# First attention batch by pairs of heads in a fused pooled-attention and MoE kernel

## The chip, the cores and the metric

The kernel runs on one core of one Trainium2 chip. The metric is the device time of one launch in microseconds. A core has five engines with their own instruction lists: TensorE (PE, matmul; its weight loads are PEld), VectorE (DVE), ScalarE (ACT), GpSimd (POOL) and SyncE (SP), which issues most of the transfers. Each list is executed in order; engines wait for one another and for transfers through semaphores.

## The reference

All data is float32. There are 8 batches, 8 heads, 576 positions, 64 features of a head; the hidden layer has 2048 features.

```python
# attention with pooled keys and values (pool = 8, so Sp = 72)
k_p = k.reshape(B, H, Sp, 8, D).mean(axis=3)
v_p = v.reshape(B, H, Sp, 8, D).mean(axis=3)
scores = 1/sqrt(D) * q @ k_p.T
scores = scores - max(scores, axis=-1)
attn = exp(scores)
attn = attn / (sum(attn, axis=-1) + 1e-09)
x = (attn @ v_p)            # transposed to [B*S, H*D] = [4608, 512]
# hidden layer and output
h = x @ w_in                # 512 x 2048
s = sin(alpha * h)
g = h + s * s / (alpha + 1e-09)
out = g @ w_out             # 2048 x 512
```

## The kernel before

The kernel has three stages. `first_batch` computes the attention of batch 0 as fast as it can. Then nine units `u` of 512 tokens of the hidden layer run, each in 28 slots of one product (a Strassen-like scheme: four groups J of w_in, seven products each; p is the number of the product). Into these slots `carry(u)` puts the attention of the next batch. Last come the output products. A product is four matmuls of 128x128 by 256, which the profile shows as eight records.

The first batch, shortened:

```python
def first_batch(self):
    far = [self.home(i, [P, 2, 2, POOL * self.D]) for i in (1, 2)]
    ...
    self.load_alpha(...); self.turn_alpha()
    for i in range(4):                          # k of batch 0, pooled on VectorE
        self.load_kv("k", 0, i, nc.vector, at=far[i // 2][:self.Sp, i % 2])
    self.root()                                 # sqrt(1/alpha): Sqrt table
    self.load_q(0)                              # q of all heads in one transfer of 1 MB
    self.load_v_rows(0, ...)
    self.load_w_in(); self.load_w_in_part(0)
    self.pairs_q(0, range(5))                   # copies q so that two heads lie side by side
    A.k_t(); A.new_a(); A.q_t(0); A.q_t(1)      # transposes of k, of q's tiles of 128 rows
    v = self.sum_v_rows(0)
    ps = A.products(0)
    A.q_t(2)
    for i in range(4):                          # by tile of 128 rows, all heads
        A.soft(i, ps)                           # maximum, exp
        if i < 3:
            ps = A.products(i + 1)
            if i < 2:
                A.q_t(i + 3)
            next(v)
        if i:
            A.norm(i - 1)                       # row sum, reciprocal, multiply on GpSimd
    A.a_t(0, 0); A.a_t(0, 1); A.norm(3); A.a_t(1, 0); A.a_t(1, 1)
    for i in range(4):
        self.load_kv("k", 1, i)                 # k of batch 1: load, pool on GpSimd
    self.load_q(1)
    self.load_w_in_part(1)
    ...                                         # a_t of tiles 2 and 3
    self.combine_w_in(0, 0); self.combine_w_in(0, 1)
    for hp in range(4):
        A.values(hp)
    self.sums_of_x(0, 0); self.sums_of_x(0, 1)
```

`load_kv` issues a transfer into one of three `kvin` buffers and adds it up in three steps on GpSimd:

```python
def load_kv(self, n, b, i, eng=None, at=None):
    t = self.kvp.tile([Sp, 2, POOL * D], F32, name="kvin") if at is None else at   # kvp: bufs=3
    nc.sync.dma_start(out=t, in_=src[b, 2 * i:2 * i + 2]...)
    for w in (4 * D, 2 * D, D):
        o = t[:, :, 0:w] if w > D else to[b][:, 2 * i:2 * i + 2, :]
        (eng or nc.gpsimd).tensor_tensor(out=o, in0=t[:, :, 0:w], in1=t[:, :, w:2 * w], op=OP.add)
```

The first slots of unit 0 (`at(slot, f, ...)` puts f ahead of the product of that slot):

```python
at(0, self.sums_of_x, u, 2); at(0, self.sums_of_x, u, 3)
at(1, lambda: A0.soft(4, A0.products(4)))       # the last 64 rows of batch 0
at(2, A0.norm, 4)
at(5, A0.a_t, 4, 0); at(5, A0.a_t, 4, 1)
at(7, A0.values_rest)
at(0, self.load_w_in_part, 2)
for J in range(1, 4):
    at((4, 10, 14)[J - 1], self.combine_w_in, J, 0)   # sums of w_in's blocks, VectorE
    at((6, 12, 15)[J - 1], self.combine_w_in, J, 1)
at(6, self.load_w_in_part, 3)
at(3, self.pairs_q, 1, (0, 1)); at(4, self.pairs_q, 1, (2, 3, 4))
for i in range(5):
    at(5 + i, A.q_t, i)
at(7, A.k_t)
...
# in hidden(): the products of the slots are p = 1, 5, 6, 2, 7, 3, 4. Left over to the next slot:
def left0(): nc.scalar.copy(out=G.b6[:], in_=G.b1[:])
def left2(): nc.scalar.copy(out=G.b7[:], in_=G.b6[:]); nc.scalar.copy(out=G.p5[:], in_=G.b5[:])
def left3(): sin(G, 0, 0, G.b1); square(G, 0, 0)
def left4(): add(G.g[:, 1, :, 1], G.b7[:], G.p5[:])   # must read b7 before p = 4 adds to it
def left5(): add(G.g[:, 0, :, 1], G.b6[:], G.p5[:]); sin(G, 1, 1, G.g[:, 1, :, 1]); ...
```

## Time and profile before

| what | value |
|---|---|
| median of 3 runs | 939.52 us (939.14 to 941.21) |
| span of the profiled execution | 937.9 us |
| first product of the hidden layer starts | 33.45 us |
| fourth k load of batch 1 issued | 32.44 us |
| VectorE's combine of w_in group 1 starts, having waited 3.00 us for a transfer | 45.22 us |
| product of slot 6 (p = 4) starts | 47.45 us |
| ScalarE table loads until 45 us | 1.18, 3.98, 17.24, 43.18 us, 1.28 us each |

A busy share is an average over stages. What bounds a stage is read from the chain that ended last, which goes back from the last instruction, at each step to what released it. `LNNN` is the line of the program; a name such as `kvin<-in_k_dram` is what is written and what is read.

### The profile page before, as it was taken

How to read it: one execution, taken by the hardware profiler on the slowest of the kernel's cores; microseconds unless marked ns; L12 is line 12 of the kernel's file. 1: busy time of each engine (PE TensorE's matmuls, PEld its weight loads, DVE VectorE, ACT ScalarE, POOL GpSimd, SP SyncE). 2: the span in 40 equal slices, each digit the busy share in tenths (PEclk: the TensorE clock that was granted, in tenths of full speed). 3: DMA queues.
4: the chain of work that ended last, by engine and by line, in shares of the span. 5: the costliest groups of instructions: out<-in, count | busy, mean ns of one | idle time of the engine just before them, and what ended most of it. 6: DMA issues, size and time to landing. Idle time of an engine off the chain costs nothing.

```text
span 937.9 us, 17446 instructions
## 1 busy us (share of the span) xinstructions
PE 916.1 (98%) x6819; PEld 814.8 (87%) x6819; DVE 691.3 (74%) x1036; ACT 444.3 (47%) x1022; POOL 200.1 (21%) x216
## 2 busy tenths in 40 slices
PE   5998999999999999999999999999999999999997
PEld 3687787878878788787888899999999999999997
DVE  5788574867748676483456889988889798889794
ACT  5557585775867758677696641112121111111111
POOL 1738262553625435260000000000000000000000
PEclk9999999999999999999999999999999999999999
DMA  8574557666576664745525446253535444343501
GB/s 234 158 215 145 145 156 194 200 159 191 152 187 214 140 188 113 183 139 159 215 88 170 161 140 176 78 168 86 164 90 149 106 136 118 123 131 98 155 14 38
DMA packets 139777, 137.82 MB, mean 147 GB/s; under 512 B 49024, under 2 KB 108176, under 8 KB 139696
## 3 DMA queue, kind: packets, MB, share of 16 engines
q1 hardware_dynamic: 138624, 135.53, 50.1%
q10 hardware_dynamic: 1072, 1.19, 0.5%
q8 instruction: 54, 0.88, 0.4%
q14 instruction: 27, 0.22, 0.1%
HBM read 74.46 MB, written 47.19 MB: 130 GB/s over the span
## 4 chain that ended last, share of the span: by engine, by line
PE 93%; DVE 3%; DMA 2%; ACT 1%; issue 1%; SPq 1%; POOL 0%; DVEq 0%; ACTq 0%; POOLq 0%
PE bank L484 44%; PE bank L764 29%; PE ps_y L764 12%; PE ps_o L304 3%; PE ps_sc L210 2%; DMA q<-in_q_dram 1%; DMA a<-in_moe_w_in_dram 1%; PE ps_qt L191 1%; PE ps_at L261 0%; DVE sm L251 0%; DVE h L463 0%; PE ps_or L313 0%; PE bank L122 0%; DVE as L366 0%; DVE a L366 0%
## 5 line engine op out<-in xcount | busy, mean ns | idle before, releaser
L484 PE MATMUL bank<-home,a 128*128 128x256 f32 x1152 | 267.1, 383 | 2.3 <-DVE h L463 1.5
L484 PEld LDWEIGHTS bank<-home,a 128*128 128x128 f32 x1152 | 214.8, 190 | 37.3 <-DVE h L463 3.6
L484 PE MATMUL bank<-home,as 128*128 128x256 f32 x864 | 202.2, 382 | 0.2
L484 PEld LDWEIGHTS bank<-home,as 128*128 128x128 f32 x864 | 161.3, 190 | 25.1 <-ACT bank L510 3.0
L107 POOL TENSOR_TENSOR kvin<-kvin 72x512 f32<-72x512 f32 x112 | 123.2, 1100 | 162.7 <-DMA kvin<-in_v_dram 106.5
L764 PE MATMUL bank<-s,wb 128*128 128x144 f32 x896 | 119.4, 286 | 0.4 <-ACT bank L877 0.4
L764 PEld LDWEIGHTS bank<-s,wb 128*128 128x128 f32 x896 | 113.7, 190 | 0.7 <-ACT bank L877 0.6
L497 ACT ACTIVATE s<-s,c 128x256 f32<-128x256 f32 (+1 forms) x216 | 110.0, 572 | 0.0
L490 ACT ACTIVATE s<-h,al 128x256 f32<-128x256 f32 x144 | 65.3, 501 | 79.5 <-DVE h L463 79.4
L463 DVE TENSOR_TENSOR h<-bank,p 128x512 f32<-128x512 f32 x72 | 49.2, 683 | 60.1 <-ACT s L497 25.4
L877 ACT COPY bank<-bank 128x144 f32<-128x144 f32 x56 | 14.7, 263 | 145.7 <-PE bank L764 144.3
L490 ACT ACTIVATE s<-bank,al 128x256 f32<-128x256 f32 x144 | 60.0, 467 | 33.8 <-PE bank L484 10.5
L551 DVE TENSOR_TENSOR h<-bank,s 128x512 f32<-128x512 f32 x36 | 24.6, 684 | 49.1 <-ACT s L497 48.4
L244 POOL TENSOR_TENSOR ex<-ex,sm 128x576 f32<-128x576 f32 (+1 forms) x40 | 45.0, 1149 | 55.5 <-DVE sm L243 30.7
L896 ACT COPY bank<-bank 128x144 f32<-128x144 f32 x56 | 14.7, 263 | 88.5 <-PE bank L764 88.5
L719 DVE TENSOR_TENSOR s<-r 128x576 f32<-128x576 f32 x64 | 48.1, 752 | 0.8
L551 DVE TENSOR_TENSOR h<-h,s 128x1024 f32<-128x1024 f32 x36 | 46.5, 1292 | 0.0
L719 DVE TENSOR_TENSOR s<-x 128x576 f32<-128x576 f32 x48 | 36.2, 754 | 7.6 <-PE ps_y L764 6.7
L854 ACT COPY bank<-ps_y 128x288 f32<-128x288 f32 x56 | 21.5, 383 | 38.7 <-PE ps_y L764 38.7
L147 DVE STREAM_TRANSPOSE tr<-q 128x1024 f32<-128x1024 f32 (+1 forms) x24 | 18.1, 808 | 27.3 <-DMA g_bridge<-h 16.3
L764 PE MATMUL ps_y<-r,wb 128*128 128x144 f32 x256 | 36.6, 286 | 0.0
L764 PE MATMUL bank<-r,wb 128*128 128x144 f32 x256 | 36.6, 286 | 0.0
(138 smaller groups left out, 1415.3 us busy)
## 6 DMA issues: line engine op xcount, KB each, us to landing
g_bridge<-h SPq DMA_DIRECT2D x72, 512.0 KB
r<-g_bridge SPq DMA_DIRECT2D x31, 1152.0 KB
out_dram<-o SPq DMA_DIRECT2D x128, 72.0 KB
q<-in_q_dram SPq DMA_DIRECT2D x8, 1024.0 KB
kvin<-in_k_dram SPq DMA_DIRECT2D x28, 288.0 KB
kvin<-in_v_dram SPq DMA_DIRECT2D x28, 288.0 KB
a<-in_moe_w_in_dram SPq DMA_DIRECT2D x16, 256.0 KB
q<-tr SPq DMA_DIRECT2D x48, 80.0 KB
```

Source lines behind the costliest of these rows:

```text
L107: (eng or nc.gpsimd).tensor_tensor(out=o, in0=t[:, :, 0:w], in1=t[:, :, w:2 * w], op=OP.add)
L210: nc.tensor.matmul(ps[e][r:r + q.shape[-1], hp, :], q[s], kb[s, hp, :], start=True, stop=True)
L244: eng.tensor_tensor(out=E(n, i, 0, H), in0=E(n, i, 0, H), in1=sm[:n].unsqueeze(2).to_broadcast([n, H, Sp]), op=OP.mult)
L304: nc.tensor.matmul(ps[64 * e:64 * e + 64, :], vp[:, h, :], x, start=True, stop=True)
L463: add = lambda o, x, y: nc.vector.tensor_tensor(out=o, in0=x, in1=y, op=OP.add)
L484: nc.tensor.matmul(ps[:, jj, :], self.A[p][:, kk, f * P:(f + 1) * P], x[:, kk, :], start=(start and jj == 0 and kk == 0), stop=(kk == 1), ...
L490: nc.scalar.activation(out=G.s[:, i, jj, j, :], in_=src[:, jj], func=AF.Sin, scale=self.al[:, f:f + 1])
L497: nc.scalar.activation(out=x, in_=x, func=AF.Square, scale=self.c[:, f:f + 1])
L551: add = lambda o, x, y: self.nc.vector.tensor_tensor(out=o, in0=x, in1=y, op=OP.add)
L719: tt = lambda o, x, y, op: nc.vector.tensor_tensor(out=o, in0=x, in1=y, op=op)
L764: nc.tensor.matmul(out, W[:, J // 2, J % 2, :], A[:, J, :], start=(start and J == 0), stop=(J == self.NJ - 1), skip_group_check=True)
L854: nc.scalar.copy(out=x0[:], in_=yz[:, 0:1, :].to_broadcast([P, 2, T]))
```

## The change

Batch 0 is worked pair of heads by pair of heads instead of tile of rows by tile of rows, so that work can begin when the first pair of k and q has landed. k and q are loaded in turn, two heads each. k is pooled into two copies side by side, on VectorE for pairs 0 and 1 and on GpSimd for pairs 2 and 3, so that q can be transposed as it lies, without the copies of `pairs_q`. The scores of a pair lie in two neighbouring banks and are handled by one maximum, one subtraction and one exp. The exp table is loaded at once, by an exp of a constant; the root of alpha, with the Sqrt table, moves into slot 3 of unit 0. A few matmuls of the identity keep TensorE busy early. The first hidden product comes before values of pairs 2 and 3. q of batch 1 is loaded earlier, k of batch 1 and groups 1 and 2 of w_in later, in slot 2. All of PSUM is one tile of eight banks that the kernel numbers itself.

```diff
@@ first_batch
+        one = self.sm.tile([P, 1], F32, name="one")
+        nc.scalar.activation(out=one[:], in_=self.ident[:, 0:1], func=AF.Exp)
+        warm = lambda n, i: [nc.tensor.matmul(self.psum([P, P], i), self.ident[:], self.ident[:], ...) for _ in range(n)]
+        warm(3, 3)
         self.turn_alpha()
-        for i in range(4):
-            self.load_kv("k", 0, i, nc.vector, at=far[i // 2][:self.Sp, i % 2])
-        self.root()
-        self.load_q(0)
+        ...
+        self.new_q(0)
+        for hp in range(4):
+            self.load_k_twice(hp, nc.vector if hp < 2 else nc.gpsimd, far[hp // 2][:self.Sp, hp % 2])
+            self.load_q_heads(0, 2 * hp, 2 * hp + 2)
         self.load_v_rows(0, h[0][:], self.tp.tile([P, self.DM], F32, name="p5")[:])
         self.load_w_in()
         self.load_w_in_part(0)
-        self.pairs_q(0, range(5))
...
+        self.load_q_rest(0, self.q_rest)
+        warm(4, 3)
+        A.q_head(0)
+        A.k_head(0)
+        for hp in range(4):
+            A.products_head(hp)
+            if hp < 3:
+                warm(1, 1 + (hp + 1) % 2)
+                A.q_head(hp + 1)
+                A.k_head(hp + 1)
+            A.soft_head(hp)
+            if hp:
+                A.norm_head(hp - 1, nc.vector if hp == 1 else nc.gpsimd)
         self.load_q(1)
-        self.load_w_in_part(1)
+        A.norm_head(3, nc.vector)
+        self.sum_v_rows(0, 0, v)
+        A.a_head(0, (1, 2))
+        self.sum_v_rows(0, 1, v)
+        A.a_head(1, (7, 2))
+        A.values(0)
+        A.values(1)
+        A.a_head(2, (2, 7))
+        A.a_head(3, (5, 6))
+        self.sums_of_x(0, 0)
         self.combine_w_in(0, 0)
         self.combine_w_in(0, 1)
-        for hp in range(4):
-            A.values(hp)
-        self.sums_of_x(0, 0)
-        self.sums_of_x(0, 1)
@@ carry, u == 0
-            at(1, lambda: A0.soft(4, A0.products(4)))
+            at(1, A0.values, 2)
+            at(1, A0.values, 3)
+            at(1, self.sums_of_x, 0, 1)
+            at(1, A0.rest_q)
+            at(2, A0.score, 4)
+            at(2, A0.exp, 4)
+            at(2, self.sums_of_x, 0, 2)
+            at(2, self.sums_of_x, 0, 3)
             at(2, A0.norm, 4)
+            for i in range(4):
+                at(2, self.load_kv, "k", 1, i)
+            at(2, self.load_w_in_part, 1)
+            at(2, self.load_w_in_part, 2)
+            at(3, self.root)
             at(5, A0.a_t, 4, 0)
             at(5, A0.a_t, 4, 1)
             at(7, A0.values_rest)
-            at(0, self.load_w_in_part, 2)
@@ attention: one pair of heads
+        def soft_head(hp):
+            ps = self.pair.pop(hp)                       # two banks, [P, 2, 4, Sp]
+            nc.vector.tensor_reduce(out=mx[:], in_=ps, axis=AX, op=OP.max)
+            nc.vector.tensor_tensor(out=x..., in0=ps, in1=mx[:].unsqueeze(3).to_broadcast([P, 2, 4, Sp]), op=OP.subtract)
+            nc.scalar.activation(out=x, in_=x, func=AF.Exp, scale=scale)
...
@@ run
-            self.ps_m = pool(top, "ps_m", 1, space=PSUM)
+            self.PS = pool(top, "ps", 1, space=PSUM).tile([P, 8, 512], F32, name="PS")
...
-                self.ps_a = pool(att, "ps_a", 3, space=PSUM)
...
-                        self.ps_y = pool(top, "ps_y", 3, space=PSUM)
```

## The prediction

> **What bounds the kernel now.** I read the page first: the busy line, the TensorE row of the 40 slices, the shares of the chain that ended last.

> ```profile
> PE 916.1 (98%) x6819; PEld 814.8 (87%) x6819; DVE 691.3 (74%) x1036; ACT 444.3 (47%) x1022; POOL 200.1 (21%) x216
> ...
> PE   5998999999999999999999999999999999999997
> ...
> PE 93%; DVE 3%; DMA 2%; ACT 1%; issue 1%; SPq 1%; POOL 0%; DVEq 0%; ACTq 0%; POOLq 0%
> ```

> TensorE sets the end: 93% of the chain. Its one poor slice is the first. So the change, which reworks the first batch, can win at most the time in which TensorE does not yet run at its pace. Next the chain in order of time, cut to the start and to 34 to 50 us; columns are start, length, what ran.

> ```profile
> 2.46 9.58 DMA q<-in_q_dram
> 12.04 0.02 issue
> 12.07 0.44 DVE q L93
> 12.50 0.04 issue
> 12.55 1.97 PE ps_qt L191 x8
> ...
> 34.57 0.90 SPq L360
> 35.46 0.04 issue
> 35.51 1.34 SPq L360
> 36.85 0.04 issue
> 36.90 8.23 DMA a<-in_moe_w_in_dram
> ...
> 45.83 0.68 DVE h L463
> 46.51 0.34 DVE aT L263
> 46.85 0.14 issue
> 46.98 0.63 PE ps_qt L191 x4
> 47.61 1.73 PE bank L484 x8
> ```

> Two absolute times anchor the kernel. One is q's landing at 12.04. The other is easy to miss: the second group (J=1) of w_in lands at 45.12, VectorE then runs its combine and an addition, and TensorE goes on with the product of slot 6 (p=4) at 47.45. After that the chain is TensorE and VectorE with no transfer for the rest of the hidden layer's first unit. A gain before 45 us counts only if this landing moves too. Why it is so late: the timeline of the SyncE queue, then of GpSimd (start, length, engine, line, what).

> ```profile
> 13.63 19.11 SPq L102 DMA_DIRECT2D kvin<-in_k_dram  x4
> 32.92 0.95 SPq L74 DMA_DIRECT2D q<-in_q_dram  x1
> 33.92 0.60 SPq L76 DMA_DIRECT2D q<-in_q_dram  x1
> 34.57 11.66 SPq L360 DMA_DIRECT2D a<-in_moe_w_in_dram  x12
> ```

> ```profile
> 28.47 3.08 POOL L107 TENSOR_TENSOR kvin<-kvin 72x512 f32<-72x512 f32 x2
> 31.63 0.78 POOL L107 TENSOR_TENSOR kp<-kvin 72x128 f32<-72x128 f32 x1
> ```

> There are three kvin buffers. The fourth load of k for batch 1 waits until GpSimd has pooled the first pair (done 32.41), and everything behind it in SyncE's queue, q of batch 1 and the w_in groups, waits with it.

> [...] the 128x512 tensor_tensor takes 0.68 us alone (45.22, 48.55) and 1.10, 0.94, 1.75 from 31 to 34 us, while GpSimd pools; GpSimd's two pooling steps take 2.06 alone and 2.84 to 3.08 there. [...] The trace shows 1.28 us (17.24 to 18.52) and the activation at 18.54[...]; I use 1.28. [...] By the windows 2.36 MB had moved at about 11 us and q landed at 12.04[...].

> **The change, part by part.** Landings: k pairs and q pairs alternate on the queue. From the 2 us windows the bytes moved are 0.48 MB by 4 us, 0.97 by 6, 1.53 by 8, 2.07 by 10, 2.64 by 12, 3.2 by 14. A k pair is 0.295 MB and a q pair 0.262, so with 1.1 to 1.5 us of lag (k's first landing 4.25) the estimates are: k 4.2, 6.8, 8.9, 11.0; q 5.5, 7.8, 9.9, 12.0; v halves 14.3 and 16.3; w_in's first group 20.

> Pair work. TensorE: four q transposes 0.66 to 0.98, two of k 0.25, sixteen score matmuls 0.7. ScalarE: copies 0.59 and 0.26. VectorE per pair: a maximum over 576 elements 0.75 (the sums of 584 take that), a subtraction 0.7, a sum 0.75, a reciprocal 0.15. The exp of 576 is 0.6 on ScalarE against 1.3 before for a tile (four of 72 and one of 288). VectorE pools pairs 0 and 1 (1.5 each); GpSimd pairs 2 and 3 at 2.06 + 0.75 = 2.8 each, so from 8.9 to 11.8 and 14.7. That makes pair 3 the last: scores end about 16.3. Pairs 0 to 2 lie beside transfers and other pairs.

> From there TensorE runs almost without a gap to the first hidden product: v sums twice 2.33 (as 4.67 before), eight transposes 1.05 four times, two of the values at 0.95: 10.8 us, so the first product starts at about 27.1 against 33.45 (probabilities of the last pair are ready near 21.3, early enough). That is 6.3 us earlier. Of it 2.3 comes back: values 2 and 3 (1.9) and the last q tile's transposes (0.4) now lie after the first product. The net lead on TensorE is about 4 us.

> Slots 0 to 3 then run: product 27.1 to 29.0; values 2, 3 and the rest of q to 31.4; product 33.3; scores of the last tile 33.9; product 35.8. VectorE subtracts the maxima to 35.7, makes two sums of x to 36.9, and the row sum and reciprocal to 37.8. The root now lies here as well: a Sqrt table load and a Sin load, 1.28 each, beside TensorE. ScalarE's chain (copies of b7 and p5 to 37.2, Sqrt to 38.7, two q copies, Sin load to 41.1, sines, squares and q copies to 44.5) lets the second q transposes go near 45. That is still ahead of 46.98, so alone it would leave 2 us of gain.

> But the other anchor moves. In the changed program GpSimd's list is: the multiplication of the last tile, then the pooling of k for batch 1. SyncE's list is: four k loads, then w_in groups 1 and 2. The multiplication waits for the reciprocal at 37.8 and ends at 39.0 (1.15). The first pair is pooled by 41.5 (2.06 + 0.45, no contention). Only then can the fourth k load be issued, 9 us later than 32.44. q of batch 1 (1.18 MB) no longer stands between, having been loaded before, near 14 us. The bytes from that load to the third transfer of the group are 0.295 + 0.786 = 1.08 MB. From a quiet queue such an amount took about 7 us at the start (0.74 to about 7.7), and at 76.94 the two stores and one k pair, 1.34 MB, took 6.8. I take 6.5: the group lands at 48.0. In VectorE's list its combine still stands ahead of the addition that slot 6's product waits for: 0.1 + 0.6 + 0.7, so that product starts at 49.4 against 47.45.

> Sum: 6.3 earlier at the first product, less 2.3 moved behind it, less about 6 of new TensorE waiting in slot 6, makes 1.9 later. From there both programs do the same work in the same order, so the shift stays. I take 0.1 to 0.2 off for same-engine waits of TensorE on older banks, 81 in the program before and 1 after, whose cost the trace does not show (a product after scores takes 1.92, one without 1.73). 939.52 + 1.8 gives 941.3.

> **Rivals.** First, the start's gain stays whole: TensorE was the bound, so its 4 us carry through to about 935.5. For it: 93% of the chain, and nothing else in the first 33 us is missing. Against it: the chain itself names the landing at 45.12, and the list order that gates its issue. I give it 0.12, with all partial gains. Second, the start hardly shortens, because the transposes of probabilities wait for VectorE, GpSimd pools pair 3 slower than 2.8 (contention gave 3.9), and ScalarE takes its copies and exps in a fixed order: the first product at 29, the multiplication 2 us later, the landing near 50, the end near 943.5. For it: VectorE's 11 us of pair work starts only after 8.8. Against: its four 1.4 us stages fit before TensorE's 10.8 us. 0.2. Third, ScalarE becomes the bound in slots 3 to 8, as Sqrt must wait for VectorE's reciprocal, and its second table load delays sines: about 1 us more. For it: ScalarE is full from 40 to 52 us before. Against: under my times it idles from 44.9 until VectorE's addition at 49.4. 0.1.

> **Range and chances.** The multiplication's start is uncertain by 1 us, the transfer time by 1, the rest by 0.5: about 1.5 in all. Allowing a longer tail for a landing I have placed too late, eight in ten: 938.6 to 944.0. Two per cent is 18.8 us; the whole start before the first product is 33 us, and most of it is real work, so within 2% is near certain: faster 0.01, same 0.98, slower 0.01.

> **What would show it.** Right: the first hidden product near 27; GpSimd's pooling of batch 1 after its 64x576 multiplication, near 39; the fourth k load issued near 41.5; the chain passing through a<-in_moe_w_in_dram again, landing near 48; TensorE idle 3 to 5 us before the product of slot 6. Wrong: that landing below 46 (then the end is below 939.5), no idle time of TensorE there, or a first product after 29. A difference that grows after 100 us would refute the statement that nothing else changes.

## The result, and the profile after

| | median of the executions | range |
|---|---|---|
| before | 939.33 us | 938.0 to 941.21 |
| changed | 945.77 us | 944.29 to 950.92 |

The ratio is 1.0073, 95% interval 1.0044 to 1.0102. The prediction was 941.3 us with a range of 938.6 to 944.0. The direction is right, the size is not: 6.4 us lost instead of 1.8, and the measured median lies outside the range. The loss is 0.7%, inside the 2% that the prediction called near certain. The spread is new as well: four executions of the changed kernel span 6.6 us.

The page of the changed kernel, the same three parts as before:

```profile
PE 920.3 (98%) x6853; PEld 820.5 (87%) x6853; DVE 686.6 (73%) x1025; ACT 441.0 (47%) x1005; POOL 200.4 (21%) x220
...
PE   7898999999999999999999999999999999999997
...
PE 89%; DVE 3%; DMA 2%; ACT 1%; SPq 1%; POOL 1%; issue 1%; DVEq 0%; ACTq 0%; POOLq 0%
```

The first slice of TensorE has risen from 5 to 7, as the change intended, and the second has fallen from 9 to 8: the hole has moved. TensorE's busy time is 4.2 us more (920.3 against 916.1) for 34 more records. That alone says nothing: twenty of these records are the fills of the first batch (matmuls whose results nobody reads), 5.2 us in all.

The chain of the changed kernel, in order of time, between 37 and 56 us (start, length, what):

```profile
37.76 1.14 POOL ex L246
38.90 1.24 POOL kvin L114
...
41.05 0.49 POOL kp L114
...
41.56 0.30 SPq L109
...
42.85 4.62 DMA a<-in_moe_w_in_dram
...
47.56 0.20 DVE as L446
...
48.32 0.69 DVE h L559
...
49.05 3.45 PE PS L580 x8
```

This is the chain that the prediction described: GpSimd's multiplication, the pooling of the first pair of k, the fourth k load, w_in, VectorE, the product of slot 6. The predicted times were 37.8 for the multiplication, 41.5 for the load, 48.0 for the landing (here 47.47) and 49.4 for the product. All are met within 0.6 us. What was not predicted stands in the last line: that product takes 3.45 us. In the kernel before it took 1.89.

Five lines of the timeline of TensorE in the changed kernel say where the rest went (start, length, what, and in brackets the idle time before it with what ended it):

```profile
26.98 1.89 PE L580 MATMUL PS<-home,a 128*128 128x256 f32 x8
44.60 0.66 PE L205 MATMUL PS<-ident,q 128*128 128x128 f32 x4 [2.63 <-ACT aT L266]
49.05 3.45 PE L580 MATMUL PS<-home,a 128*128 128x256 f32 x8 [3.80 <-DVE h L559]
53.80 1.94 PE L580 MATMUL PS<-home,a 128*128 128x256 f32 x8
...
91.85 0.63 PE L263 MATMUL PS<-ident,ex 128*72 128x128 f32 x4 [1.86 <-ACT aT L268]
```

The same points in the kernel before (its second transposes of q in slot 6 start at 46.98):

```profile
33.45 1.99 PE L484 MATMUL bank<-home,a 128*128 128x256 f32 x8
47.45 1.89 PE L484 MATMUL bank<-home,a 128*128 128x256 f32 x8
50.63 1.94 PE L484 MATMUL bank<-home,a 128*128 128x256 f32 x8
...
87.32 0.63 PE L261 MATMUL ps_at<-ident,ex 128*72 128x128 f32 x4 [0.34 <-DVE aT L263]
```

So the changed kernel is 6.5 us ahead at the first product, 1.6 behind at the product of slot 6, 3.2 behind at the product of slot 7, and 4.5 behind at the sixth group of a_t transposes, where it waits 1.86 us for a bank of PSUM (a_t are the transposes of the probabilities); the kernel before waited 0.34 us there. After that nothing is added: the spans end 4.6 us apart (942.5 and 937.9). The prediction had the shift constant from slot 6 on.

The windows of the same profile, for TensorE alone (window, its length, busy time with records, granted TensorE clock, share of the DMA engines, GB/s), explain the long product:

```profile
44.00:46.00 2.00, 0.66 (x4) 0.80 1.06 322
46.00:48.00 2.00, 0.00 (x0) 0.50 0.99 327
48.00:50.00 2.00, 0.95 (x2) 0.50 1.07 350
50.00:52.00 2.00, 2.00 (x6) 0.50 1.11 361
52.00:54.00 2.00, 2.00 (x27) 0.99 1.05 301
```

TensorE has 0.66 us of work between 41.97 and 49.05. Its clock falls to 0.50 at about 45.2 (an estimate from the mean of 0.80 for 44 to 46), after the wait of 2.63 us for a copy of ScalarE and before most of the wait for w_in. It is 0.50 through that wait, and the product that ends it takes 3.45 us instead of 1.89. The clock is back at 1.00 at about 52.0 (from the mean of 0.99 for 52 to 54), 3 us after the product began.

### The profile page after: what moved, and what is told of

Same layout as the page of the kernel before. It is cut to its first block, busy times and chain, and to the rows that moved or that the text cites. A ratio compares the mean times of both kernels' runs of the same rounds, so it can differ in the third digit from the quotient of the medians.

```text
span 942.5 us, 17456 instructions
## 1 busy us (share of the span) xinstructions
PE 920.3 (98%) x6853; PEld 820.5 (87%) x6853; DVE 686.6 (73%) x1025; ACT 441.0 (47%) x1005; POOL 200.4 (21%) x220
## 3 DMA queue, kind: packets, MB, share of 16 engines
q1 hardware_dynamic: 138688, 135.53, 49.5%
## 4 chain that ended last, share of the span: by engine, by line
PE 89%; DVE 3%; DMA 2%; ACT 1%; SPq 1%; POOL 1%; issue 1%; DVEq 0%; ACTq 0%; POOLq 0%
PE PS L580 42%; PE PS L874 40%; PE PS L382 3%; PE PS L224 2%; DMA g_bridge<-h 1%; SPq L356 1%; DMA home<-in_k_dram 1%; ACT s L593 1%; DVE h L559 1%; DMA a<-in_moe_w_in_dram 0%; DVE as L446 0%; DVE tr L347 0%; DVE sm L253 0%; POOL home L121 0%; PE PS L339 0%
## 5 line engine op out<-in xcount | busy, mean ns | idle before, releaser
L580 PE MATMUL PS<-home,a 128*128 128x256 f32 x1152 | 268.2, 384 | 5.5 <-DVE h L559 4.9
L580 PEld LDWEIGHTS PS<-home,a 128*128 128x128 f32 x1152 | 215.9, 191 | 40.0 <-DVE h L559 7.2
L580 PE MATMUL PS<-home,as 128*128 128x256 f32 x864 | 202.4, 382 | 0.3 <-ACT PS L606 0.2
L580 PEld LDWEIGHTS PS<-home,as 128*128 128x128 f32 x864 | 161.3, 190 | 25.1 <-ACT PS L606 3.1
L874 PE MATMUL PS<-s,wb 128*128 128x144 f32 x896 | 119.4, 286 | 0.4 <-ACT PS L987 0.4
L874 PEld LDWEIGHTS PS<-s,wb 128*128 128x128 f32 x896 | 113.7, 190 | 0.7 <-ACT PS L987 0.6
L987 ACT COPY PS<-PS 128x144 f32<-128x144 f32 x56 | 14.7, 263 | 145.7 <-PE PS L874 144.3
L874 PE MATMUL PS<-r,wb 128*128 128x144 f32 x512 | 73.2, 286 | 0.0
L874 PE MATMUL PS<-s,a 128*128 128x144 f32 x512 | 73.2, 286 | 0.0
L874 PEld LDWEIGHTS PS<-r,wb 128*128 128x128 f32 x512 | 67.1, 190 | 0.1
L874 PEld LDWEIGHTS PS<-s,a 128*128 128x128 f32 x512 | 67.1, 190 | 0.0
L1006 ACT COPY PS<-PS 128x144 f32<-128x144 f32 x56 | 14.7, 263 | 88.5 <-PE PS L874 88.5
```

The lines of the kernel that those rows point to most:

```text
L580: nc.tensor.matmul(ps[:, jj, :], self.A[p][:, kk, f * P:(f + 1) * P], x[:, kk, :], start=(start and jj == 0 and kk == 0), stop=(kk == 1), ...
L874: nc.tensor.matmul(out, W[:, J // 2, J % 2, :], A[:, J, :], start=(start and J == 0), stop=(J == self.NJ - 1), skip_group_check=True)
L987: nc.scalar.copy(out=x1[:, 0, :], in_=x0[:, 1, :])
L1006: nc.scalar.copy(out=x1[:, 1, :], in_=x1[:, 0, :])
```

## Experiments

Three terms had to be told apart, with the late w_in as the predicted fourth. **The clock**: with the idle time in slot 6 it falls from 1.00 to 0.50. **The banks**: in the changed kernel the transposes of q, of k and of the probabilities take three banks of PSUM in strict turn (`abank`), so that one of them can wait for a bank that ScalarE frees late although another is free. **The start**: with the few fills of the first batch the start takes two courses, called warm and cold here. In a warm start the scores of a pair take 0.73 us on TensorE, in a cold one 1.24.

All medians stand beside runs of the kernel before on the same chip, whose medians were 939.9 to 940.3 us. They come from four chips: the rows from a_busy to a_w1_ring; a_nowarm, a_hot, a_hot_busy and a_early_hot; the other rows that begin with a; and those that begin with e. A difference of medians across these groups can be off by some tenths of a microsecond.

| kernel | what is different from the changed kernel | median (range; n), us | ratio to before, 95% |
|---|---|---|---|
| a_busy | fills in slot 6 | 946.03 (943.56 to 947.91; 6) | 1.0064 [1.0050, 1.0078] |
| a_w1first | w_in group 1 ahead of k | 946.84 (943.51 to 948.64; 6) | 1.0070 [1.0053, 1.0088] |
| a_ring | banks by hand | 947.38 (944.35 to 950.89; 6) | 1.0075 [1.0055, 1.0095] |
| a_w1_ring | both | 945.43 (940.75 to 947.11; 9) | 1.0047 [1.0030, 1.0065] |
| a_nowarm | no fills at the start | 948.89 (947.60 to 949.17; 4) | 1.0095 [1.0081, 1.0109] |
| a_hot | more fills at the start | 946.34 (943.65 to 946.96; 5) | 1.0065 [1.0053, 1.0078] |
| a_hot_busy | a_hot and a_busy | 943.72 (943.17 to 945.14; 5) | 1.0044 [1.0030, 1.0058] |
| a_hot_ring | a_hot and a_ring | 944.94 (942.84 to 947.80; 5) | 1.0044 [1.0032, 1.0057] |
| a_hot_busy_ring | all three | 943.53 (941.82 to 945.16; 5) | 1.0033 [1.0021, 1.0045] |
| a_hot_busy_w1_ring | all three, and w_in first | 941.10 (940.52 to 943.00; 13) | 1.0015 [1.0007, 1.0023] |
| a_early | k and w_in loaded in the first batch, banks by hand | 940.58 (937.72 to 943.14; 14) | 1.0002 [0.9992, 1.0012] |
| a_early_hot | a_early and a_hot | 937.43 (937.27 to 938.04; 10) | 0.9974 [0.9965, 0.9983] |
| e_turn | a_early_hot, banks in turn again | 940.48 (939.51 to 942.36; 13) | 1.0004 [0.9996, 1.0012] |
| e_k_only | a_early_hot, w_in behind the k loads again | 937.62 (937.42 to 938.17; 9) | 0.9974 [0.9964, 0.9983] |
| e_w_only | a_early_hot, k late again | 942.67 (942.21 to 943.67; 8) | 1.0028 [1.0018, 1.0038] |
| e_cold | a_early_hot, no fills at the start | 939.26 (938.33 to 940.53; 13) | 0.9992 [0.9984, 1.0001] |

### One term at a time in the changed kernel

**a_busy**: 24 small matmuls that nobody reads fill TensorE's idle time in slot 6.

```diff
+fill = lambda n: [nc.tensor.matmul(self.psum([P, P], 2), self.ident[:], self.ident[:], ...) for _ in range(n)]
+at(6, fill, 8)
 for i in range(5):
     at(5 + i, A.q_t, i)
+at(6, fill, 16)
```

> The changed kernel with 24 more matmuls of the identity (128x128) in slot 6 of unit 0: 8 before and 16 after the second q transposes, where TensorE stood idle for 2.6 and 3.8 us. Theory (the idle time halves TensorE's clock): granted clock 1.0 from 44 to 54 us, the product of slot 6 takes 1.9 us and not 3.4, its start stays near 49.0 because the w_in transfer gates it, and the time falls by 1.6 us, to about 944. Rival (the half clock has another cause, such as the load of transfers, and is not tied to idle time): the product still takes 3.4 us, the time stays or grows.

Measured 946.03 us. In the profile the clock is 1.00 in every window from 44 to 54 us, though the transfers are as dense there (share 1.07 to 1.10 from 44 to 52 us), and the product is short again. TensorE's timeline of a_busy:

```profile
50.31 1.99 PE L580 MATMUL PS<-home,a 128*128 128x256 f32 x8 [1.07 <-DVE h L559]
53.60 1.94 PE L580 MATMUL PS<-home,a 128*128 128x256 f32 x8
```

So the half clock goes with the idle time: 0.50 without the fills, 1.00 with them. But in this execution VectorE's addition came 1.26 us later than in the profile of the changed kernel (49.58 against 48.32; w_in's transfer took 5.18 us instead of 4.62; in a_hot, which has no fills in slot 6, that product came as late, at 50.05), and the product of slot 7 stands where it stood (53.60 against 53.80). The median, expected near 944, can't confirm the size of the term: the start scatters more than the term is worth.

**a_w1first**: w_in's second group is issued ahead of the four k loads of slot 2.

```diff
+at(2, self.load_w_in_part, 1)
 for i in range(4):
     at(2, self.load_kv, "k", 1, i)
-at(2, self.load_w_in_part, 1)
 at(2, self.load_w_in_part, 2)
```

> The changed kernel with w_in group 1 loaded ahead of the four k loads in slot 2, so that its transfer doesn't queue behind the fourth k load. Theory (the transfer that lands at 47.5 is the wait that replaced q's landing): group 1 lands before 30 us, VectorE's combine runs near 41.3, the product of slot 6 starts near 45 and not 49.05 at full clock, and then the k transposes of slot 7 wait for GpSimd's pooling until 49.5 to 51; the time falls by 3 us (2 to 4.5), to about 943. Rival (ScalarE, with its Sqrt load and copies, is the bound in slots 3 to 8): the product of slot 6 starts at 48 or later and the time falls by less than 1 us.

Measured 946.84 us. No gain in the median, where 3 us were expected; the profiled execution had a cold start (scores 1.24 us in all four pairs, first product at 31.34 instead of 26.98). Its product of slot 6 started at 49.61, which taken alone is the rival's sign (ScalarE as the bound). It is 4.4 us of late start: in a_w1_ring, below, with a warm start, the same product came at 45.63, near the 45 of the theory.

**a_ring**: the banks of batch 1's a_t groups are given by hand, so that no group gets the bank that ScalarE frees last.

```diff
-ps = self.abank([Sp, 4, P])
+ps = self.abank([Sp, 4, P], (5, 6, 7, 6, 5, 6, 6, 7, 5, 6)[2 * i + g] if b == 1 else None)
```

> The changed kernel with the banks of batch 1's transposed probabilities given in the order that reuses the bank that VectorE frees, instead of the strict turn of three. Theory (the strict turn makes the sixth group wait for a ScalarE copy that stands behind four squares): TensorE's wait of 1.86 us near 90 us shrinks to 0.4, the time falls by 1.5 us, to about 944.3. Rival (the wait is hidden by a later wait anyway): it falls by less than 0.5 us.

Measured 947.38 us. The wait is gone, the time is not less. The lines of TensorE in a_ring:

```profile
7.73 1.24 PE L311 MATMUL PS<-tr,q 64*64 64x72 f32 x32 [0.62 <-ACT tr L280]
31.39 1.89 PE L582 MATMUL PS<-home,a 128*128 128x256 f32 x8
53.51 3.78 PE L582 MATMUL PS<-home,a 128*128 128x256 f32 x8 [3.67 <-DVE h L561]
98.08 0.63 PE L263 MATMUL PS<-ident,ex 128*72 128x128 f32 x4 [0.34 <-DVE aT L268]
```

The last line waits 0.34 us for VectorE, as in the kernel before, instead of 1.86 us. The first line shows why that did not help here. The same score matmuls, at the same 7.73 us, take 0.73 us in the profile of the changed kernel:

```profile
7.73 0.73 PE L311 MATMUL PS<-tr,q 64*64 64x72 f32 x32 [0.61 <-ACT tr L280]
```

In a_ring all four pairs' scores took 1.24 us, and the first hidden product came 4.4 us later. The two programs are the same up to that point. So one program can start warm or cold, and much of the noise is there.

**a_w1_ring**: the edits of a_w1first and a_ring, as above.

> The two edits together (w_in group 1 ahead of the k loads, and the order of banks). Theory (they act in different slots and add): 4.5 us less than the changed kernel, about 941.3, near the kernel before. Rival (one hides the other): no more than the better of the two alone.

Measured 945.43 us, from 940.75 to 947.11. The profiled execution took 941.65 us and had a warm start (first product at 27.11). With w_in early, TensorE waits in slot 6 for a copy of ScalarE, since q's transposes still take the banks in turn, and in slot 7 for GpSimd's pooling of k. The first wait is enough for the clock, which falls to 0.50 at about 44.2 (an estimate from the mean of 0.56 for 44 to 46), 2.2 us after TensorE's last work ended at 42.09; w_in has no part in it. TensorE in a_w1_ring:

```profile
44.72 1.11 PE L205 MATMUL PS<-ident,q 128*128 128x128 f32 x4 [2.63 <-ACT aT L266]
45.63 2.90 PE L582 MATMUL PS<-home,a 128*128 128x256 f32 x8
...
51.61 0.28 PE L194 MATMUL PS<-ident,kp 72*128 72x72 f32 x1 [1.68 <-POOL kp L114]
```

### The start

**a_nowarm**: the changed kernel without the ten fill matmuls of the first batch.

```diff
-warm = lambda n, i: [nc.tensor.matmul(...) for _ in range(n)]
+warm = lambda n, i: [nc.tensor.matmul(...) for _ in range(0 * n)]
```

> The changed kernel without its ten matmuls of the identity in the first batch. Theory (the spread of the changed kernel's times, 944 to 951, is TensorE's clock in the first 22 us: where the early work fills it without a gap it runs full from about 8 us on, otherwise at half until about 22 us, which starts the first hidden product at 31.4 and not 27.0): the slow start in every execution, transposes of a q pair 1.06 us and scores 1.24 in all four pairs, first hidden product at 30 to 32, times of 947 to 951 with little below. Rival (the spread is of the transfers or of the slot-6 wait): the same mixture as with them, lowest time near 944.

Measured 948.89 us, and all four executions lie between 947.60 and 949.17. Without fills the start is cold: all four pairs' scores took 1.24 us and the first product began at 30.61. The slow end of the changed kernel's spread fits this course; its slow executions were not profiled, and the slowest, 950.92, lies above all four.

**a_hot**: more fills, ahead of each pair's scores.

```diff
 for hp in range(4):
+    warm(2, 1 + (hp + 1) % 2)
     A.products_head(hp)
```

> The changed kernel with two more identity matmuls ahead of each pair's scores, in the 0.6 us in which TensorE waits for ScalarE's copies. Theory (clock at the start): full clock from 8 us in every execution, scores 0.73 us, first hidden product at 27 to 27.5, times within 2 us of each other near 944.5 (what is left over 939.9 is the gated transfer, the half clock in slot 6 and the turn of banks). Rival: the times still spread from 944 to 951.

Measured 946.34 us, not near 944.5, with 3.3 us between the executions instead of 2. The profiled execution started warm (first product at 27.17) and still took 946.34. Most of its further delay against the profile of the changed kernel is in slot 6. TensorE in a_hot:

```profile
50.05 3.78 PE L580 MATMUL PS<-home,a 128*128 128x256 f32 x8 [4.48 <-DVE h L559]
53.76 1.12 PE L392 MATMUL PS<-aT,vp 72*64 72x64 f32 x16
54.81 0.93 PE L205 MATMUL PS<-ident,q 128*128 128x128 f32 x4
```

The clock was 0.50 from 46 to 54 us and 0.65 on average from 54 to 56: product, values and most of the transposes of slot 6 ran at 0.50 (in the changed kernel the latter two take 0.69 and 0.66, at a clock of 0.99), and the product of slot 7 came at 55.83, 2.03 us later than in the profile of the changed kernel: 0.19 from the start, 0.81 from the rest of the way to slot 6, 1.03 from the longer half clock. From the start of slot 6's product to that of slot 7's it takes 5.78 us, where the kernel before takes 3.18: the half clock costs 2.60 us in this execution and 1.57 in that of the changed kernel (4.75). It varies by when the clock comes back: at about 52.0 in the changed kernel, about 55.4 in a_hot (from the mean of 0.65).

**a_hot_busy**: a_hot, with the fills of a_busy in slot 6.

> The start kept busy as above, and the 24 identity matmuls in slot 6 of unit 0 besides. Theory: against the kernel with the busy start alone the product of slot 6 takes 1.9 us and not 3.4, and the time is lower by 1 to 1.6 us, about 943. Rival (half clock in slot 6 costs nothing in the end): the same time as with the busy start alone.

Measured 943.72 us, 2.6 less than a_hot; the ranges still overlap between 943.65 and 945.14. Slot 6 ran at clock 1.00, its product took 1.99. The difference of the medians is the 2.60 us of a_hot's profile, by luck as much as by measure, for the five executions of each scatter by 2 to 3 us, and the profiled one of a_hot_busy lost 2.2 us at the start. A spread of 2 us remains: in the profiled execution a transfer of k had come later, GpSimd's first pooling started at 10.57 instead of 9.03 us, TensorE waited 1.15 us for it, the clock fell to 0.50 at 14 to 16 us and the third pair's scores took 1.24. More fills alone did not hold this start.

### The terms together

These three add edits whose diffs stand above.

**a_hot_ring**: the edits of a_hot and a_ring.

> The fills that keep the start warm, and the hand-given banks for batch 1's a_t groups. Theory (three terms that the prediction lacked: half clock in slot 6, the turn of the three banks, the cold start; they add): the kernel with the fills alone took 946.34; its sixth a_t group waited 1.86 us for the ScalarE, which should fall to about 0.3, so 944.8 (943.8 to 945.6). The slot-6 product stays near 3.5 us. Rival (the wait for the bank only moves to a later wait): 946.3.

Measured 944.94 us, 1.4 less than a_hot, as the bank's wait is worth (1.86 less 0.34). The ranges overlap widely, so this run alone does not prove it. The profiled execution, 947.80, went cold in spite of the fills: GpSimd's first pooling started at about 10.7 (an estimate: TensorE's wait for it ended at 13.67, and at 13.50 in a_hot_busy with its 10.57), the third pair's scores took 1.24 us, the fourth pair's transposes of q 1.06 (0.60 in a_hot), and the first product came at 30.68.

**a_hot_busy_ring**: with the fills of slot 6 too. The predicted term, the late landing, is left. (The transposes of q in slot 6 still take the banks in turn; their wait lies ahead of the wait for w_in.)

> All three terms taken away, and only the late landing of w_in left: fills at the start, fills in slot 6, banks by hand. Theory: this is the kernel that the prediction had in mind, so it should take what was predicted for the change: fills at the start and in slot 6 gave 943.72, less 1.5 for the bank, 942.2 (941.2 to 943.0), and an end about 2 to 3 us behind the kernel before. Rival (the late landing costs more than the 2 us that I gave it, and the terms found are small): 943.7 or more.

Measured 943.53 us, above what I expected, and within 0.2 of a_hot_busy. In its profile the banks' wait was 0.34 and the product of slot 6 took 1.99, but its start was half cold (the third pair's scores took 1.24 us, first product 28.80, again after a late pooling by GpSimd, at 10.02): the 1.8 us lost there went through to the end (span 941.9). Without them the 3.7 us by which slot 7 lags the kernel before would be 1.9, the loss that the prediction had.

**a_hot_busy_w1_ring**: with w_in ahead of the k loads as well.

> As before, and w_in's second group also issued ahead of the four k loads, so that its landing no longer gates slot 6. Theory: the chain then goes through the GpSimd's pooling of k; the product behind k_t was at 51.73 in the kernel with w_in first and banks by hand at half clock, with the clock held it should be near 50.5 to 51, where the kernel before had 50.63: 939.5 (938.5 to 940.8). Rival (the whole loss lies after slot 6): 942 and no less.

Measured 941.10 us, a little above the expected range. It is 2.4 us less than a_hot_busy_ring, of the order of what the late landing was to cost. The kernel before is still 1.1 us ahead. With everything undone but the new order of the first batch and the late k loads, the change had gained nothing from its 6 us at the start.

**a_early_hot**: the k loads of batch 1, but for the fourth, and w_in's second group are issued within the first batch. Banks by hand, also for q_t(1), fills as in a_hot.

```diff
 self.load_q(1)
 A.norm_head(3, nc.vector)
+for i in range(3):
+    self.load_kv("k", 1, i)
+self.load_w_in_part(1)
...
-for i in range(4):
-    at(2, self.load_kv, "k", 1, i)
-at(2, self.load_w_in_part, 1)
+at(2, self.load_kv, "k", 1, 3)
 at(2, self.load_w_in_part, 2)
...
 # q_t
-ps = self.abank([P, NP, P])
+ps = self.abank([P, NP, P], 7 if (b, i) == (1, 1) else None)
```

> The start kept busy, three of batch 1's k loads and w_in group 1 issued in the first batch behind q of batch 1 (the fourth k load stays in slot 2), GpSimd pooling them from about 26 us beside VectorE's sums of w_in, and the banks of transposed probabilities and of the second q transposes chosen so that they wait for VectorE. Theory (with the transfer, GpSimd's pooling, the clock and the banks out of the way the earlier start is kept): product of slot 6 at 43 to 45 at full clock, no wait of the k transposes for GpSimd, 4 to 6 us less than the changed kernel with the busy start, 938 to 940 or below, some 2 us under the kernel before at best. Rival (VectorE, slowed by GpSimd's pooling, holds slots 1 to 3): the product of slot 1 starts after 33 us and the time is above 941.

Measured 937.43 us, ratio 0.9974 [0.9965, 0.9983]. It beats both kernels, and all ten executions lie within 0.8 us. TensorE in a_early_hot:

```profile
41.25 0.64 PE L263 MATMUL PS<-ident,ex 64*72 64x64 f32 x8 [0.76 <-POOL ex L246]
45.45 0.63 PE L205 MATMUL PS<-ident,q 128*128 128x128 f32 x4 [1.25 <-DVE aT L266]
45.92 1.89 PE L582 MATMUL PS<-home,a 128*128 128x256 f32 x8
49.10 1.94 PE L582 MATMUL PS<-home,a 128*128 128x256 f32 x8
85.14 0.63 PE L263 MATMUL PS<-ident,ex 128*72 128x128 f32 x4 [0.34 <-DVE aT L268]
```

The longest wait in slot 6 is 1.25 us, the clock is 1.00 from 36 to 56 us, and the product of slot 7 is 1.5 us ahead of the kernel before. The span ends 1.7 us ahead.

**a_early**: the same without the fills of a_hot.

> Three k loads and w_in's second group issued within the first batch, banks by hand, but no fills at the start. Theory: the start is then warm in some executions and cold in others, so two groups of times, near 937.4 (warm) and near 941.8 (cold, 4.4 us more, the delay of the first hidden product seen in two profiles), with a median anywhere between. Rival (the early loads alone make the difference and the start hides behind them): every execution within 1 us of 937.4.

Measured 940.58 us, fourteen executions from 937.72 to 943.14. The fastest was profiled; its start was warm (scores 0.73 in all four pairs). The spread of 5.4 us becomes 0.8 with the fills, which change nothing but the start. The cold start of e_cold, below, does not account for all of it: that kernel ends no later than 940.53. The executions do not fall into two clean groups as I had expected: the start has courses between warm and cold, like the ones in a_hot_busy and a_hot_busy_ring.

### One term put back into the steady kernel

In a_early_hot the start no longer scatters, so one term at a time can be sized.

**e_turn**: the strict turn of the three banks put back (no bank by hand).

```diff
 # a_t of batch 1
-ps = self.abank([Sp, 4, P], (5, 6, 7, 6, 5, 6, 6, 7, 5, 6)[2 * i + g] if b == 1 else None)
+ps = self.abank([Sp, 4, P])
 # q_t
-ps = self.abank([P, NP, P], 7 if (b, i) == (1, 1) else None)
+ps = self.abank([P, NP, P])
```

> The best kernel so far (early loads, banks by hand, fills at the start; 937.43, 937.27 to 938.04) with the strict turn of three banks put back. Theory: the sixth a_t group waits 1.86 us instead of 0.34, nothing takes it up later, so 1.5 us more: 938.9 (938.5 to 939.8; q_t(1) in slot 6 may add up to 1 us). Rival (a wait that the later work hides): 937.4 to 937.8.

Measured 940.48 us: 3.05 more than a_early_hot, and 2.86 more than e_k_only on the same chip, twice the 1.5 that the theory gave the bank and above its range. The timeline of TensorE in e_turn shows why:

```profile
45.10 0.66 PE L205 MATMUL PS<-ident,q 128*128 128x128 f32 x4 [2.39 <-ACT aT L266]
45.59 2.75 PE L580 MATMUL PS<-home,a 128*128 128x256 f32 x8
50.33 1.94 PE L580 MATMUL PS<-home,a 128*128 128x256 f32 x8
87.86 0.63 PE L263 MATMUL PS<-ident,ex 128*72 128x128 f32 x4 [1.86 <-ACT aT L268]
```

The two copies in slot 6 that free a bank, by VectorE and by ScalarE, in the same execution:

```profile
43.13 0.41 DVE L266 COPY aT<-PS 72x256 f32<-72x256 f32 x1
44.67 0.37 ACT L266 COPY aT<-PS 72x256 f32<-72x256 f32 x1
```

And TensorE's windows (columns as above):

```profile
44.00:46.00 2.00, 0.90 (x6) 1.00 0.03 8
46.00:48.00 2.00, 2.00 (x7) 0.62 0.03 8
48.00:50.00 2.00, 2.00 (x21) 0.53 0.00 0
```

The turn does its damage twice. In slot 6 the second transposes of q wait 2.39 us for the bank that ScalarE frees at 45.04; VectorE had freed the other at 43.54, 1.5 us before. The clock falls to 0.50, the product takes 2.75, and from product to product slot 6 takes 4.74 us instead of 3.18. Against a_early_hot only 1.2 us of this are left by slot 7, because in this profile TensorE had come to the wait 1.5 us earlier (42.70 against 44.20). The sixth a_t group then adds its 1.5. So here the strict turn brings both the bank's wait and the half clock, with no late landing of w_in.

**e_k_only**: only the three k loads are early; w_in's second group stands behind the fourth k load again, in slot 2.

```diff
-self.load_w_in_part(1)          # first_batch
...
 at(2, self.load_kv, "k", 1, 3)
+at(2, self.load_w_in_part, 1)
```

> The best kernel with only the three k loads in the first batch, and w_in's second and third groups behind the fourth k load in slot 2. Theory (w_in is late because the fourth k load, ahead of it in the queue, waits until GpSimd has pooled the first, which stands behind the 64x576 multiplication): the fourth load is then free early, w_in lands some 5 us sooner, and nearly all of the gain stays: 937.8 (937.2 to 938.8). Rival (what counts is w_in's place in the queue): 941 to 943.

Measured 937.62 us: nothing is lost. SyncE's queue in e_k_only, and then in the changed kernel:

```profile
19.70 12.94 SPq L109 DMA_DIRECT2D kvin<-in_k_dram  x4
32.68 6.83 SPq L440 DMA_DIRECT2D a<-in_moe_w_in_dram  x12
```

```profile
19.41 22.45 SPq L109 DMA_DIRECT2D kvin<-in_k_dram  x4
41.90 6.91 SPq L440 DMA_DIRECT2D a<-in_moe_w_in_dram  x12
```

w_in's place in the queue is the same. What differs is the place of the poolings in GpSimd's list. Where the change put them, they follow the 64x576 multiplication (37.76 to 38.90). Emitted with the loads in the first batch, the first pooling runs at 28.16 and its buffer is free at 32.31; the fourth load goes at 32.34. The group behind it is issued 9.2 us sooner.

**e_w_only**: only w_in's second group is early; the four k loads are in slot 2.

```diff
-for i in range(3):              # first_batch
-    self.load_kv("k", 1, i)
...
-at(2, self.load_kv, "k", 1, 3)
+for i in range(4):
+    at(2, self.load_kv, "k", 1, i)
```

> The best kernel with only w_in's second group in the first batch, and the four k loads in slot 2 as in the changed kernel. Theory: w_in no longer gates slot 6, but the poolings of k still stand behind the 64x576 multiplication on GpSimd and k_t waits for them, as in the kernel with w_in first (its executions with a warm start 940.75 to 942.6): 941 (940 to 942.3). Rival (the landing of w_in is the whole loss): 937.4 to 938.2.

Measured 942.67 us, 5.2 more, and 0.4 above the range. w_in no longer gates anything: the product of slot 6 begins at 43.92. But TensorE then waits for k's pooling. Its lines in e_w_only:

```profile
49.22 0.38 PE L194 MATMUL PS<-ident,kp 72*128 72x72 f32 x1 [1.78 <-POOL kp L114]
51.77 0.38 PE L194 MATMUL PS<-ident,kp 72*128 72x72 f32 x1 [2.16 <-POOL kp L114]
51.95 3.71 PE L582 MATMUL PS<-home,a 128*128 128x256 f32 x8
```

The wait has moved from w_in to k, one slot further on, and the clock falls there (0.50 from 50 to 54 us). The landing of w_in was the visible end of the chain; the late pooling of k is its cause.

**e_cold**: a_early_hot without any fills in the first batch.

```diff
-    warm(2, 1 + (hp + 1) % 2)   # the fills of a_hot
...
-warm = lambda n, i: [nc.tensor.matmul(...) for _ in range(n)]
+warm = lambda n, i: [nc.tensor.matmul(...) for _ in range(0 * n)]
```

> The best kernel without any fill multiplications in the first batch. Theory: the start is cold in every execution, as in the changed kernel without fills (947.6 to 949.2 there, all above the median), and the first hidden product comes 3.5 to 4.4 us later: 941.5 (940.6 to 943.2) with a small spread, against 937.43 with fills. Rival (a late start hides behind transfers): 937.4 to 939.5.

Measured 939.26 us, 1.8 more; the fastest, 938.33, lies above the slowest of a_early_hot. That is less than the 4 us of the theory and inside the rival's range: the start is cold (scores 1.24 us in all four pairs, first product at 30.56 instead of 27.55), but half of it hides. Of these 3.0 us, slot 6 keeps 1.53 (47.45 against 45.92), because two waits of a_early_hot, 0.77 us for VectorE's sums of x and 0.76 for GpSimd's multiplication, vanish. Its product of slot 7 stands at 50.68, beside 50.63 in the kernel before, and both spans are 937.9.

### What the end follows

With the profiles side by side the end can be read from two numbers, the start of the product of slot 8 (53.60 before; slot 7's will not do, since in a_w1first, a_ring and e_w_only that product itself took 3.62, 3.59 and 3.71 us, against 1.94) and whether the sixth a_t group waits for the bank:

| profile | slot 8 against before | bank wait | span against before |
|---|---|---|---|
| changed | +3.16 | 1.86 | +4.6 |
| a_busy | +2.96 | 1.86 | +5.0 |
| a_w1first | +7.02 | 1.86 | +8.7 |
| a_nowarm | +7.66 | 1.86 | +9.5 |
| a_hot | +5.20 | 1.86 | +6.6 |
| a_hot_busy | +4.11 | 1.86 | +5.0 |
| e_turn | -0.31 | 1.86 | +1.1 |
| a_ring | +10.68 | 0.34 | +10.8 |
| a_w1_ring | +1.09 | 0.34 | +1.9 |
| a_hot_ring | +7.83 | 0.34 | +8.1 |
| a_hot_busy_ring | +3.71 | 0.34 | +4.0 |
| a_hot_busy_w1_ring | +1.88 | 0.34 | +1.3 |
| a_early | -2.10 | 0.34 | -2.0 |
| a_early_hot | -1.53 | 0.34 | -1.7 |
| e_k_only | -2.00 | 0.34 | -2.3 |
| e_w_only | +3.09 | 0.34 | +3.0 |
| e_cold | +0.04 | 0.34 | 0.0 |

Whatever a kernel with the banks by hand loses up to slot 8 it keeps, within 0.8 us; with the strict turn 0.9 to 2.0 come on top, 1.4 in the median of these.

## Why the prediction was wrong

**The bound, the rework of the first batch, the queue.** Right. First product predicted at 27.1, measured 26.98; the multiplication of GpSimd 37.8 and 37.76; the fourth load 41.5 and 41.56; the landing 48.0 and 47.47; the product of slot 6 at 49.4 and 49.05. The chain passes through a<-in_moe_w_in_dram again. The loss of 1.9 us at slot 6 measured 1.60. e_k_only and e_w_only bear the mechanism out: the fourth k load behind the pooling, behind the multiplication. These times are those of a warm start.

**"From there both programs do the same work in the same order, so the shift stays."** This step failed, in two places. I had counted "new TensorE waiting in slot 6" as time lost once, and left out what waiting does to TensorE afterwards: the clock fell to 0.50, and the product behind the wait took 3.45 us instead of 1.89. That is 1.57 us in the profiled execution and 2.60 in that of a_hot. Two waits make up the idle time, 2.63 us for ScalarE's copy and 3.80 for w_in; in a_w1_ring the clock falls to 0.50 with the first alone, and no run has the second alone. In the changed kernel the turn of the banks is not to blame for the first: VectorE's copy came only at 48.92. And the programs do not do the same work on the same resources: PSUM is numbered differently. The strict turn of three banks makes the sixth a_t group wait 1.86 instead of 0.34 us, 1.5 more. I had read the change of PSUM as only a relief of same-engine waits (0.1 to 0.2 us, which no run isolates). The predicted shift, measured as 1.6, plus 1.57, plus 1.5, makes 4.7; the two spans are 4.6 apart. That adds up one warm profile with itself; the other tests of the parts are a_busy for the clock (0.50 with the idle time, 1.00 with it filled; not what that costs), e_turn for the banks, and e_k_only and e_w_only for the queue.

**A constant clock at the start.** All my durations of the first batch were those of a warm start (scores 0.7 us a pair). In executions that start cold the first product comes up to 4.4 us later (31.39 in a_ring), and nothing hides it in the changed kernel, because the landing hangs on the same start. The profile of the changed kernel is of its warm course, 944.29 us, the fastest of four; the median lies 1.5 us above, the slowest 6.6 above. A prediction for one course was not one for the median. That this last 1.5 us is the cold start is likely but not shown, since no slower execution of the changed kernel was profiled.

**The rivals.** The first, a gain kept whole, did not happen: of 6.5 us nothing was left at slot 6. With the k loads early, a_early_hot keeps 2.4 us of it. The second, a first product near 29 and an end near 943.5, comes nearer to the median than the prediction, for a different reason: the start comes late where TensorE is slow (scores 1.24 us instead of 0.73), not because VectorE or GpSimd is slow. The third, ScalarE as the bound, did not happen: ScalarE ended its copy of q at 45.03 and waited 4.01 us for VectorE. But slot 6's first wait, 2.63 us, was for a copy of ScalarE, and its copies hold the banks in e_turn and a_w1_ring, so ScalarE matters as the owner of a bank.

**What would have refuted it.** A difference growing after 100 us: there was none; it grew at 49 to 53 us and at 92. The range was too narrow: it held the uncertainty of the terms that were summed (the multiplication's start, the transfer), and nothing for a term left out.

Open: what decides between a warm and a cold start from one execution to the next. A late first pooling by GpSimd, behind k's transfer, is seen in a_hot_busy (10.57 us instead of 9.03) and a_hot_busy_ring (10.02) and estimated for a_hot_ring (10.7), but a_ring was cold before its first score, with the same times as the changed kernel up to there.

## What to carry to other kernels

When work is moved earlier, look at what is issued behind it in each engine's list: here the loads' own consumers, set behind a late multiplication on GpSimd, held the buffer, the queue and the next stage. Price a new wait of TensorE like those of 2.39 and 2.63 us in slot 6 here at its length plus what the work behind it loses at a clock of 0.50, 1.56 us in e_turn and 1.57 to 2.60 behind the two waits together. And if pools of PSUM are replaced by hand-numbered banks in turn, ask for each tile which engine frees the bank it will get, not how many banks there are.

## What the runs showed of the hardware

A start with many small gaps stayed cold in a_ring: four gaps of 0.62 us, each ahead of a pair's scores. TensorE was busy 3.38 of every 4 us from 4 to 20 us and slow until about 22: the scores took 1.24 us against 0.73 in the profile of the changed kernel, the first half of v's sums, from 19.92, took 2.97 us and the second, from 24.34, 1.94. The granted clock shown for these windows is 1.00. There the durations of a known instruction say more than the clock column. The changed kernel was warm with the same 3.38 us from 4 to 8 us and a gap of 0.61. What makes the course vary from run to run is not shown here.
